# Windowed attention and a gated layer on one core: when attention weights are normalised, turned and read back

## The chip, the cores and the metric

The kernel runs on one core of a Trainium2 chip. The metric is the device time of one execution in microseconds (us). The core has engines with instruction queues of their own: TensorE (PE; its weight loads PEld) for matrix products into PSUM, VectorE (DVE), ScalarE (ACT), GpSimd (POOL), and SyncE (SP), whose queue issues the DMA transfers in the order in which the program wrote them. An engine takes its instructions in order and stops at one whose inputs are not ready.

## What is computed

Attention with two kinds of window (half the heads look at the last 32 keys, the others at every fourth of the last 128), then a gated layer. Cut to what matters:

```python
batch, n_heads, seq, head_dim = (8, 8, 576, 64)        # q, k, v
scores = np.where(masks, scale * q @ k.T, -1e9)
attn = np.exp(scores - max(scores)); attn = attn / (sum(attn) + 1e-09)
x = (attn @ v).transpose(0, 2, 1, 3).reshape(4608, 512)
h = x @ w_in                                           # w_in 512 x 2048
g = h * erf(softplus(h))
out = g @ w_out                                        # w_out 2048 x 512
```

## The kernel before

**Attention** is cut into 72 units. A unit is eight strips of 32 queries, two heads on top of each other, with 64 keys a strip. For each unit TensorE makes the scores (`scores`, L243), VectorE applies the mask and takes the maximum (`mask_max`, L254), ScalarE takes exponents and their sums (`exponents`, L264), VectorE forms the reciprocal of the sums and POOL multiplies by it (`normalize`, L275 to L277). The product with the values needs the weights turned, keys along the partitions. Units up to 17 are turned on TensorE (`turn`). Units from 18 (`LATER`) are turned another way: VectorE transposes 32x32 blocks of two units into `pT` (`swap`, L309), one DMA puts the result into DRAM (`pt<-pT`, L312, "the put"), and one DMA a unit reads it back, regrouped, into the unit's `prob` tile (`back`, L321, `prob<-pt`, "the load back"). The load back cannot go out before its put has landed. The value products (`later_values`, L332) read it.

**The layer** runs over chunks of 512 tokens. The first three chunks are done plainly, in the plain part: a loop over 48 half steps `x`, two to a pair of 128 hidden columns (`t`, `j`). A half step is, on TensorE, twelve products of the first matrix (`mm1`, L590) into PSUM bank `h` (even half steps) or `tx` (odd ones), then twelve of the second matrix two pairs behind (`mm2`, L705). VectorE copies the bank out (`take`, L662), ScalarE applies softplus and erf, VectorE multiplies and splits the result into a high and a low part (`gate`: L674, L680 `ghi`, L681 `glo`), which the `mm2` of the next half step reads. The remaining chunks come behind the plain part, in periods, which the change does not touch.

**Visits** put attention work into the loop. `visits` gives each half step its units: from half step 13 on, every odd half step up to 41 takes two units (9 takes two as well, 11 none). At the end of a visited half step TensorE does `attend`: value products of the pair whose scores were made two visits before, scores of the new pair; then ScalarE copies rows out (L386). SP gets, behind it, the next values and queries (`load_v`, L231, `load_qk`, L224), and the stores of finished rows (`store_x`, L416) and of other results.

**The way of a pair before**, with the visit in half step x: mask and maximum at its end, exponents in x + 1, normalised by VectorE and POOL in x + 2, transposed and put in x + 3, read back at the very end of x + 3, used by the visit of x + 4. Lists hold the units on the way: `todo`, `fresh` and `scaled` (to be normalised), `divided` (to be transposed), `away` (to be read back). Between the put and the load back in SP's queue stands whatever that half step issues, in half steps 8 to 22 the load of weights (`load_w`, L493, called by `prep_dve` inside `weights` once VectorE has emptied the buffer). In half step 28 `fetch_x` issues eight loads of activations (L577) early in the half step. From half step 29 on, `build` makes sums of weights for the later part (L600 to L629), with its stores (L604, L629) on SP. In half step 11 (`SAVED`) `pT` is used for something else.

Of the kernel before, what the change touches and what calls it, by code (L numbers as in the profile page):

```python
# [62 lines left out]
NT = len(STEPS)  # L63
# [9 lines left out]
SAVED = 2 * (HALF + 1) + 1  # L73
# [21 lines left out]
LATER = 2 * NBLK  # L95
# [67 lines left out]
def attn_moe_kernel(ctx: ExitStack, tc: tile.TileContext, qk, v, masks, eye, w_in, w_out, out):  # L163
# [57 lines left out]
    def load_qk(u):  # L221
        if u < NU:
            n = QW + key_start(u, SPU - 1) + KEYS
            nc.sync.dma_start(out=qkz[u % 2][:, 0:n], in_=qk[u, :, 0:n])  # L224
# [46 lines left out]
    def normalize(u):  # L271
        rinv = small.tile([P, 2 * PARTS], F32, name="rinv")

        if u >= FIRST:
            nc.vector.tensor_scalar(sums[u], sums[u], 1.0e-9, None, op0=ALU.add)  # L275
        nc.vector.reciprocal(out=rinv, in_=sums.pop(u))
        nc.gpsimd.tensor_tensor(probs[u], probs[u], rinv.broadcast_to([P, 2 * PARTS, KEYS]), op=ALU.mult)  # L277
        if u >= LATER:
            divided.append(u)
# [19 lines left out]
    def swaps():  # L299
        if divided:  # L300
            swap(list(divided))
            divided.clear()

    def swap(units):

        m = len(units)
        t = pz[1][:, 0:m * 2 * P].rearrange("p (b u n) -> p b u n", b=2, u=m)
        for i, u in enumerate(units):
            nc.vector.transpose(out=t[:, :, i].rearrange("p b (g q) -> p g b q", g=2 * PARTS),  # L309
                                in_=probs[u].rearrange("p g (b k) -> p g b k", b=2))  # L310
        put = dram.tile([2, P, m, P], F32, name=f"pt{units[0]}")
        nc.sync.dma_start(out=put.rearrange("s (r b) u n -> (s r) (b u n)", b=2),  # L312
                          in_=t.rearrange("p b u n -> p (b u n)"))
        away.extend((u, put[:, :, i]) for i, u in enumerate(units))
# [3 lines left out]
    def back():  # L318
        while away:
            u, put = away.pop(0)  # L320
            nc.sync.dma_start(out=probs[u].rearrange("p (s g) k -> p s (g k)", s=2),  # L321
                              in_=put.rearrange("s p n -> p s n"))
# [95 lines left out]
    def has(u):  # L418
        return 0 <= u < NU
# [3 lines left out]
    def busy(k):  # L423

        for _ in range(k):
            nc.tensor.matmul(h, idle[:, 0:P], idle, start=True, stop=True)

    def first_visit(n):

        m = n - LAG  # L430
        copy = nc.scalar.copy if 1 <= n <= EARLY else nc.vector.tensor_copy
        if has(m):
            transposes(m)
        scores(n)
        load_qk(n + 2)
        busy(2 if has(m) else 6)
        if has(m):
            turned(m, copy)
        if 1 <= n <= EARLY:
            prep_act()  # L440
        if has(m):
            values(m)
            busy(2)
        if has(n - 2):
            normalize(n - 2)
        mask_max(n)
        part_lo()
        if has(m):
            rows(m)
            finish(m)  # L450
        if m == NBLK - 1:
            part_lo()
        exponents(n)
        load_v(n - 1)
# [34 lines left out]
    def load_w(i):  # L489
        if prep:  # L490
            _, src, hi, lo = prep.pop(0)
            d = doubles(i)
            nc.sync.dma_start(out=d, in_=src.bitcast(I32).rearrange("p (n w) -> p n w", w=2))  # L493
            staged.append((i, d, hi, lo))
# [346 lines left out]
    for p in (1, 2, 3):  # L841
        j = i - 13 + p
# [542 lines left out]
    with tc.manual_schedule():  # L1385
        nc.gpsimd.memset(idle, 1.0)
        busy(8)
        load_qk(0)
        nc.sync.dma_start(out=cst[:, 0:NMASK * KEYS], in_=masks)
        load_qk(1)  # L1390
        nc.sync.dma_start(out=ident, in_=eye)
        for n in range(FIRST):
            if n < 3:
                load_w(n)
            first_visit(n)
            if 1 <= n <= EARLY:
                prep_dve()
        normalize(FIRST - 2)
        part_lo()

        plan, late = visits()


        pause = SAVED + 1,

        def weights(x):
            if x not in pause:
                prep_act()
                prep_dve(keep=2 if SAVED - 4 < x <= SAVED else None)

        due = {n - LAG: x for x, ns in plan.items() for n in ns if n < LATER + LAG}
        todo, scaled, fresh = [], [FIRST - 1], []
        for x in range(2 * NT):
            t, j = divmod(x, 2)
            ns = plan.get(x, [])
            scored, ready = [n for n in ns if has(n)], ready_of(ns)
            second.update(ready[1:])

            if t < 2:
                turn(ready)  # L1420
                weights(x)
            if t < NT:
                after = STEPS[t + 1][0] if ends(t) and t + 1 < NT else None
                if x == 2 * HALF - 4:
                    load_x(1, range(twice))
                elif x == 4 * SPC - 4:
                    fetch_x(2)
                if x == SAVED:
                    hold(True)
                mm1(t, j)  # L1430
                if x == 0:
                    for cc in range(twice, CC):
                        nc.sync.dma_start(out=x0[cc - twice], in_=xs[cc].bitcast(F32)[:, :, 0:TOK])
                part_lo()
                if not late_take(t, j):
                    take(t, j)
                if after is not None and j == PAIR - 1:
                    load_x(after, range(twice, CC))
                    part_lo()

            if x == 1 or j == 0 and x:
                for u in todo:
                    exponents(u)
                fresh, todo = todo, []
            if late_take(t, j):
                take(t, j)
            if j == 1 and 1 <= t <= NT:
                table(t - 1)
            if t < 2:
                attend(ready, scored)  # L1450
            if t >= 2:
                turn(ready)
                if j == 0 and x < 2 * NT - 4:
                    swaps()

            while scaled:
                normalize(scaled.pop(0))
            scaled, fresh = fresh, []
            if j == 1 and 1 <= t <= NT:
                gate(t - 1, 0)  # L1460
            if j == 0 and 2 <= t:
                gate(t - 2, 1)
            if j == 1 and t < NT:
                argument(t)
            if t >= 2:
                if x != SAVED:
                    weights(x)
                mm2(t - 2, j)
                if x == SAVED:
                    save()  # L1470
                    weights(x)
                    hold(False)
                    load_w(2)
                elif ends(t - 2):
                    if j == 1:
                        store(STEPS[t - 2][0])
                    elif STEPS[t - 2][2] == 2:
                        fetch()
            if t >= 2:
                attend(ready, scored)  # L1480
            def at_once():
                for u in [u for u in scaled if due.get(u) == x + 1]:
                    scaled.remove(u)
                    normalize(u)

            def load_units():
                for n in ns:
                    soon(load_v, n - 1 - (n >= LATER + LAG))
                    soon(load_qk, n + 2)

            sooner = BUILD <= x < PACE[-1]
            if sooner:
                load_units()
            load_left(t + 2, j)
            jobs(FORE.get(x, ()))
            build(x, at_once if x > BUILD else (lambda: None))
            if not sooner:
                load_units()
            back()
            for n in scored:  # L1500
                mask_max(n)
                todo.append(n)
            if x == 4 * SPC - 2:
                load_x(2, range(twice))
            at_once()
            for m in ready:
                finish(m)
        assert not todo and not scaled and len(divided) <= 2
        for i in range(len(ITEMS)):
            period(i, late)  # L1510
        for d in range(FIN * SPC, DOUBLES * SPC):
            final(d)
        rest_steps()
        for s in range(len(LASTS)):
            sums_step(s)
        assert not pending and not prep and not staged and not begun and not made and not rest
# [86 lines left out]
```

## Time and profile before

| | before |
|---|---|
| median of 3 runs | 910.04 us (906.52 to 912.1) |
| profiled execution: its own time | 910.9 us |
| its span, first to last instruction | 909.1 us |
| TensorE busy | 861.3 us (95%) |
| VectorE, ScalarE, POOL busy | 696.0, 608.3, 87.3 us |
| mean granted clock of TensorE, as a share of full speed | 0.983 |
| moved by DMA | 207.72 MB, 228 GB/s |

The profile is of one execution. "A <- B" in a wait means that A stood idle until B was done. Matrix products are pipelined, so a line of several shows the time they occupy together. Times in the rows below are counted from the start of the span.

### The profile page before, as it was taken

What the parts mean: (1) busy time and instruction counts of PE and PEld (TensorE: products, weight loads), DVE (VectorE), ACT (ScalarE), POOL (GpSimd) and SP (SyncE); (2) the same over time, 40 slices, a digit from 0 to 9 for tenths busy, and PEclk for the clock granted to TensorE, in tenths of its full rate; (3) what the DMA queues carried; (4) which work ended last, traced back from release to release, by engine and by line L of the source; (5) the groups of instructions that cost most, each with busy time, mean ns of one, the idle gap of its engine ahead of it and who ended that gap; (6) DMA issues with size and microseconds to landing.
All of it is one profiled execution on the core that took longest, in us unless ns stands there. A gap on an engine that the chain in (4) does not pass through costs nothing.

```text
span 909.1 us, 21921 instructions
## 1 busy us (share of the span) xinstructions
PE 861.3 (95%) x8302; PEld 707.4 (78%) x8314; DVE 696.0 (77%) x1748; ACT 608.3 (67%) x1358; POOL 87.3 (10%) x97
## 2 busy tenths in 40 slices
PE   7799899889979799999999999999999999999998
PEld 3467788677867678878888878888788888889998
DVE  5888888768658688978677767586788768878895
ACT  6889879776858578766676843567456547776442
POOL 2322111112111111001111100010000000000000
PEclk9999999989989899999999999999999999999999
DMA  8874446465648979867786792567668638999541
GB/s 288 286 258 135 150 155 223 150 212 160 214 154 275 314 234 329 310 202 266 264 264 228 252 319 93 160 252 246 203 192 285 240 115 312 324 315 379 187 147 47
DMA packets 102425, 207.72 MB, mean 228 GB/s; under 512 B 10416, under 2 KB 41648, under 8 KB 99248
## 3 DMA queue, kind: packets, MB, share of 16 engines
q1 hardware_dynamic: 99360, 197.88, 64.8%
q10 hardware_dynamic: 2960, 8.46, 2.3%
q8 instruction: 65, 1.06, 0.5%
q14 instruction: 40, 0.33, 0.1%
HBM read 141.54 MB, written 64.75 MB: 227 GB/s over the span
## 4 chain that ended last, share of the span: by engine, by line
PE 49%; DVE 2%; DMA 2%; issue 0%; ACT 0%; SPq 0%; DVEq 0%
PE acc L705 16%; PE h L865 8%; PE tx L865 8%; PE sp L865 6%; PE acc L1231 4%; PE sp L1231 2%; PE tx L1231 1%; PE h L1231 1%; PE sp L332 1%; DMA win<-xT 1%; PE sp L243 1%; DMA prob<-pt 1%; DMA out_dram<-w 1%; DVE glo L681 0%; DVE rows L1062 0%
## 5 line engine op out<-in xcount | busy, mean ns | idle before, releaser
L705 PE MATMUL acc<-wout_hi,ghi 128*128 128x512 f32 x448 | 174.9, 391 | 0.2 <-DVE o L744 0.2
L705 PE MATMUL acc<-wout_lo,ghi 128*128 128x512 f32 x448 | 174.4, 389 | 0.0
L705 PE MATMUL acc<-wout_hi,glo 128*128 128x512 f32 x448 | 123.8, 389 | 1.6 <-DVE glo L681 1.6
L277 POOL TENSOR_TENSOR prob<-prob,rinv 128x256 f32<-128x256 f32 x72 | 77.6, 1092 | 494.0 <-DVE ssum L275 326.5
L264 ACT ACTIVATE prob<-prob,nmax 128x64 f32<-128x64 f32 x288 | 96.3, 337 | 7.9 <-DVE nmax L254 4.1
L705 PEld LDWEIGHTS acc<-wout_hi,glo 128*128 128x128 f32 x448 | 84.0, 188 | 19.5 <-DVE glo L681 2.0
L705 PEld LDWEIGHTS acc<-wout_hi,ghi 128*128 128x128 f32 x448 | 84.1, 188 | 18.6 <-DVE ghi L680 0.7
L705 PEld LDWEIGHTS acc<-wout_lo,ghi 128*128 128x128 f32 x448 | 84.1, 188 | 17.3
L254 DVE CUSTOM_DVE_ANT_0 prob<-sp,cst 128x64 f32<-128x64 f32 x288 | 45.2, 219 | 53.5 <-ACT rows L386 41.2
L914 ACT ACT_TABLE_LOAD x26 | 33.4, 1283 | 46.2 <-DVE hc L882 23.7
L386 ACT COPY rows<-sp 128x128 f32<-128x128 f32 (+7 forms) x167 | 27.6, 306 | 48.2 <-PE sp L243 47.7
L332 PEld LDWEIGHTS sp<-prob,v 64*64 64x64 f32 x1728 | 30.7, 145 | 35.1 <-issue 29.3
L332 PE MATMUL sp<-prob,v 64*64 64x32 f32 x1728 | 33.8, 229 | 24.8 <-DMA prob<-pt 21.1
L865 PE MATMUL tx<-win 128*128 128x512 f32 x216 | 55.9, 394 | 0.2 <-DVE hc L884 0.2
L865 PE MATMUL h<-win 128*128 128x512 f32 x216 | 55.9, 394 | 0.2 <-DVE dbl L884 0.2
L264 ACT ACTIVATION_READ_ACCUMULATOR prob<-prob,nmax 128x1 f32 x288 | 54.4, 189 | 0.0
L590 PE MATMUL h<-x,win 128*128 128x512 f32 x192 | 51.1, 409 | 1.0 <-issue 1.0
L590 PE MATMUL tx<-x,win 128*128 128x512 f32 x192 | 48.0, 392 | 0.0
L865 PEld LDWEIGHTS h<-win 128*128 128x128 f32 x216 | 39.9, 188 | 9.8 <-DVE dbl L884 1.3
L865 PEld LDWEIGHTS tx<-win 128*128 128x128 f32 x216 | 39.9, 188 | 9.6 <-DVE hc L884 0.9
L590 PEld LDWEIGHTS h<-x,win 128*128 128x128 f32 x192 | 37.4, 199 | 9.9 <-issue 1.3
L590 PEld LDWEIGHTS tx<-x,win 128*128 128x128 f32 x192 | 35.7, 188 | 7.5
(312 smaller groups left out, 1912.2 us busy)
## 6 DMA issues: line engine op xcount, KB each, us to landing
win<-ws SPq DMA_DIRECT2D x24, 1024.0 KB, 5.2
v<-in_v_dram SPq DMA_DIRECT2D x72, 256.0 KB, 4.8
win<-ws SPq DMA_DIRECT2D x24, 768.0 KB, 5.8
qk<-in_qk_dram SPq DMA_DIRECT2D x48, 272.0 KB, 4.8
dbl<-in_w_in_dram SPq DMA_DIRECT2D x16, 512.0 KB, 4.3
dbl<-in_w_out_dram SPq DMA_DIRECT2D x16, 512.0 KB, 4.2
ws<-x SPq DMA_DIRECT2D x32, 256.0 KB, 5.2
win<-wd SPq DMA_DIRECT2D x14, 512.0 KB, 8.4
```

Source lines behind the costliest of these rows:

```text
L243: nc.tensor.matmul(sps[h][r * STRIP:(r + 1) * STRIP, i, p, :], qkz[i][hs, s * STRIP:(s + 1) * STRIP], qkz[i][hs, at:at + KEYS], start=True ...
L254: nc.vector.tensor_tensor_reduce(out=pr[:, g, :], in0=sps[h][:, u % 2, p, :], in1=mask[QUADS.index(kinds(u, p))], scale=-SCALE, scalar=HUG ...
L264: nc.scalar.activation(out=probs[u][:, j, :], in_=probs[u][:, j, :], func=AF.Exp, scale=-1.0, bias=nmax[:, j:j + 1], accum_out=sums[u][:, ...
L277: nc.gpsimd.tensor_tensor(probs[u], probs[u], rinv.broadcast_to([P, 2 * PARTS, KEYS]), op=ALU.mult)
L332: nc.tensor.matmul(xp[h * D:(h + 1) * D, qs], vt[ks, s, h, :], w[ks, s % 2, h, s // 2 ^ p, :], start=True, stop=True, tile_position=(p * K ...
L386: nc.scalar.copy(out=to, in_=src)
L590: nc.tensor.matmul((h, bank)[j], win_at[:, ftp, j, cc // 2, w, cc % 2, :], x[cc], start=(k == 0 and i == 0), stop=(k == CC - 1 and i == 2))
L705: nc.tensor.matmul(args["out"], args["lhsT"], args["rhs"], start=args["start"], stop=args["stop"])
L865: nc.tensor.matmul(bank_, w[:, wi, c, :], x[c][:, xi, :], start=(c == 0 and n == 0), stop=(c == 1 and n == 2))
L914: nc.scalar.activation(out=l, in_=e, func=AF.Softplus)
L1231: nc.tensor.matmul(y, x[:, at_], w, start=(q == 0 and j == 0 and n == 0 and s % 2 == 0), stop=(q == QUART - 1 and j == 1 and n == 2), skip ...
```

## The change

Three edits, all in the loop of the plain part. First, in an even half step, units from 18 on are normalised at once, at the end of the half step that made their exponents (x + 1; from half step 30 on ahead of the sums of L609), and no longer after the copy of `tx` in x + 2. Second, `swaps` (the transposes and the put) is called in odd half steps, x + 2, behind that copy; not in half step 11, and not from half step 43 on. A pair visited in half step 9 is therefore put in 13 where it was put in 12. Third, `back` is called in even half steps, x + 3, behind the first products and ahead of `weights`, and no longer as the last but one thing of each half step. The visit that uses the weights stays x + 4.

```diff
             if t >= 2:
                 turn(ready)
-                if j == 0 and x < 2 * NT - 4:
+                if j and x != SAVED and x < 2 * NT - 5:
                     swaps()
+                elif j == 0:
+                    back()
...
             def at_once():
-                for u in [u for u in scaled if due.get(u) == x + 1]:
+                for u in [u for u in scaled if due.get(u) == x + 1 or u >= LATER and j == 0]:
                     scaled.remove(u)
                     normalize(u)
...
             if not sooner:
                 load_units()
-            back()
             for n in scored:
                 mask_max(n)
                 todo.append(n)
```

SP's queue in half steps 16 and 17, as a piece of the difference (- before, + now). `pt_2298` is the put that before went out in half step 16; `pt_2160` is the one of the same pair of units now, put in half step 15; `dbl` are loads of weights:

```order
 L224 DMA qk_83<-in_qk_dram 128x544
 L416 DMA xT_103<-rows 128x576
-L312 DMA pt_2298<-pT_88 128x512
-L493 DMA dbl_2311<-in_w_out_dram 128x1024
-L321 DMA prob<-pt_2298 128x2x128 x2
-L493 DMA dbl_2362<-in_w_out_dram 128x1024
+L321 DMA prob<-pt_2160 128x2x128 x2
+L493 DMA dbl_2313<-in_w_out_dram 128x1024
+L312 DMA pt_2351<-pT_88 128x512
+L493 DMA dbl_2366<-in_w_out_dram 128x1024
```

The load back has come up to right behind the store of rows, ahead of the load of weights, and the next pair's put stands between the two loads of weights.

SP's queue in half step 28, before (a load of activations is the last of eight):

```order
L577 DMA w<-xT_102 128x128
L577 DMA w<-xT_103 128x384
L312 DMA pt_3450<-pT_88 128x512
L321 DMA prob<-pt_3450 128x2x128 x2
L231 DMA v_86<-in_v_dram 128x512
L224 DMA qk_84<-in_qk_dram 128x544
```

and now:

```order
L577 DMA w<-xT_102 128x128
L577 DMA w<-xT_103 128x384
L321 DMA prob<-pt_3293 128x2x128 x2
L312 DMA pt_3494<-pT_88 128x512
L231 DMA v_86<-in_v_dram 128x512
L224 DMA qk_84<-in_qk_dram 128x544
```

The load back passes a put, but the eight loads of activations stay ahead of it.

VectorE in half steps 18 and 19 before, from the copy of bank `h` on (`win` and `w` are the preparing of weights, `ssum` and `rinv` the normalising):

```order
L662 COPY hc<-h 128x512
L309 STREAM_TRANSPOSE pT_88<-prob 128x4x2x32 x2
L680 CAST ghi<-s 128x512
L681 TENSOR_TENSOR glo<-s,ghi 128x512
L522 TENSOR_TENSOR win<-w,win 128x4x128
L526 TENSOR_SCALAR w<-w 128x512
L527 SCALAR_TENSOR_TENSOR w<-dbl_2171,w 128x512
L528 SCALAR_TENSOR_TENSOR w<-dbl_2171,w 128x512
L662 COPY hc<-tx 128x512
L275 TENSOR_SCALAR ssum<-ssum 128x4
L276 RECIPROCAL rinv<-ssum 128x4
```

and now, from the low part `glo` on:

```order
L681 TENSOR_TENSOR glo<-s,ghi 128x512
L522 TENSOR_TENSOR win<-w,win 128x4x128
L526 TENSOR_SCALAR w<-w 128x512
L527 SCALAR_TENSOR_TENSOR w<-dbl_2175,w 128x512
L528 SCALAR_TENSOR_TENSOR w<-dbl_2175,w 128x512
L275 TENSOR_SCALAR ssum<-ssum 128x4
L276 RECIPROCAL rinv<-ssum 128x4
L275 TENSOR_SCALAR ssum<-ssum 128x4
L276 RECIPROCAL rinv<-ssum 128x4
L662 COPY hc<-tx 128x512
L309 STREAM_TRANSPOSE pT_88<-prob 128x4x2x32 x2
L674 TENSOR_TENSOR s<-hc,s 128x1024
```

The normalising has moved ahead of the copy of `tx`, and the transposes from behind the copy of `h` to behind the copy of `tx`, between it and the product `s`.

## Rows read from the trace of the kernel before

**Rows 1.** Waits of TensorE, whole run: waiter, releaser: us in total, times, longest.
```profile
PE sp L332 <- DMA prob<-pt: 21.1, 7, 5.4
PE sp L332 <- issue: 3.4, 2, 2.9
PE h L590 <- issue: 1.0, 1, 1.0
```

**Rows 2.** Timeline of TensorE, value products: start, us, operation, [idle before <-releaser].
```profile
108.16 0.89 PE L332 MATMUL sp<-prob,v 64*64 64x32 f32 x32 [2.87 <-issue]
...
161.80 1.56 PE L332 MATMUL sp<-prob,v 64*64 64x32 f32 x64 [2.89 <-DMA prob<-pt]
...
177.89 1.14 PE L332 MATMUL sp<-prob,v 64*64 64x32 f32 x64 [1.39 <-DMA prob<-pt]
...
194.03 1.93 PE L332 MATMUL sp<-prob,v 64*64 64x32 f32 x64 [3.11 <-DMA prob<-pt]
...
255.30 1.93 PE L332 MATMUL sp<-prob,v 64*64 64x32 f32 x64 [5.44 <-DMA prob<-pt]
...
303.81 1.93 PE L332 MATMUL sp<-prob,v 64*64 64x32 f32 x64 [5.10 <-DMA prob<-pt]
```

**Rows 3.** Busy times by stretch: length, engines' busy us, granted clock, DMA share, GB/s.
```profile
108.16:347.24 239.08, 216.72 (x2657) 177.43 (x2657) 178.37 (x548) 176.80 (x453) 34.52 (x30) 0.94 0.64 211
177.89:194.03 16.14, 13.03 (x177) 10.68 (x177) 13.94 (x41) 12.32 (x33) 2.35 (x2) 0.99 0.60 184
194.03:209.77 15.74, 15.74 (x177) 12.88 (x177) 9.14 (x34) 10.11 (x28) 1.38 (x1) 0.79 0.57 169
223.84:236.81 12.97, 12.97 (x177) 10.65 (x176) 8.81 (x32) 10.22 (x28) 2.35 (x3) 1.00 0.50 149
285.67:303.81 18.14, 13.05 (x176) 10.68 (x177) 14.39 (x40) 11.05 (x28) 2.35 (x2) 0.98 0.89 309
```

**Rows 4.** Timeline of SP's queue, half steps 7, 8, 15 and 16: start, us, transfer issued.
```profile
99.35 0.33 SPq L493 DMA_DIRECT2D dbl<-in_w_in_dram  x1
...
104.52 0.90 SPq L321 DMA_DIRECT2D prob<-pt  x2
...
152.26 0.42 SPq L416 DMA_DIRECT2D xT<-rows  x1
152.77 0.38 SPq L312 DMA_DIRECT2D pt<-pT  x1
...
159.03 0.88 SPq L321 DMA_DIRECT2D prob<-pt  x2
```

**Rows 5.** Lines L321 (first) and L312, 85 to 375 us: landing times.
```profile
DMA to landing us min/median/max: 2.0/2.7/5.8
...
DMA to landing us min/median/max: 1.7/3.8/7.3
```

**Rows 6.** Waits of SP's queue, whole run: us in total, times, longest.
```profile
SPq L321 <- DMA pt<-pT: 29.4, 13, 3.6
```

**Rows 7.** Timelines of VectorE, POOL and TensorE, half steps 15 to 17.
```profile
146.41 0.98 DVE L681 TENSOR_TENSOR glo<-s,ghi 128x512 fp32r<-128x512 f32 x1
...
152.56 0.69 DVE L681 TENSOR_TENSOR glo<-s,ghi 128x512 fp32r<-128x512 f32 x1
...
156.23 0.69 DVE L662 COPY hc<-tx 128x512 f32<-128x512 f32 x1 [0.59 <-PE tx L590]
...
157.47 2.35 POOL L277 TENSOR_TENSOR prob<-prob,rinv 128x256 f32<-128x256 f32 x2 [10.63 <-DVE ssum L275]
...
152.40 1.07 PE L705 MATMUL acc<-wout_hi,glo 128*128 128x512 f32 x4
```

**Rows 8.** Timeline of SP's queue, half steps 28 and 35.
```profile
246.76 2.19 SPq L577 DMA_DIRECT2D w<-xT  x4
249.04 0.38 SPq L312 DMA_DIRECT2D pt<-pT  x1
252.86 0.88 SPq L321 DMA_DIRECT2D prob<-pt  x2
...
300.79 2.12 SPq L746 DMA_DIRECT2D out_dram<-w  x4
```

## The prediction, made before the changed kernel ran

> **What bounds the kernel now.** I read the views in this order. First TensorE's waits: over the whole run it waits 21.1 us, in seven places, for one thing, the load that brings turned attention weights back (`prob<-pt`), and next to nothing else; 2.9 us at the same line are put down to "issue" [rows 1]. All of these lie in the plain part. The timeline then gives the places: the value products (L332) of the visits that start at 108.16 (the "issue" one: its load back was issued only at 104.52), 161.80, 177.89, 194.03, 255.30 and 303.81 us, and two more that share the remaining 3.2 us [rows 1, 2, 4]. Then busy times from visit to visit. A visit comes every second half step; where nothing is late, as from 223.84 us, two half steps take 12.97 us and TensorE is busy for all of it [rows 3]. So TensorE sets the pace, and a wait of TensorE is paid in full. The stretches show a second loss. Behind the wait of 1.39 us the granted clock is 0.99 over the stretch; behind the one of 3.11 us it is 0.79, and the stretch takes 15.74 us with TensorE busy throughout, 2.77 us too long [rows 2, 3]. That is time at the lower level (1.2 GHz in place of 2.4); the clock fell only after the long waits.
>
> **How much there is to win.** From 108.16 to 347.24 us, the first and the last visit of the plain part that read returned weights, there are 16 pairs of half steps. Fourteen should take 14 x 12.97 = 181.6 us. The first two pairs hold one visit, with half the value products (12.97 less half of 1.14 is 12.4, and 12.97 less a visit of 1.95 is 11.0): 23.4. Together 205.0, and they take 239.08: 34.1 too long. With the first wait, 2.87, the loss is 37.0 us: 24.0 of waits for the load back, 1.0 for another load (L590), and 12 of low clock [rows 1, 2, 3].
>
> **What the change moves.** Nothing is added or taken away: each pair of units keeps two normalisations, two multiplies on POOL, two transposes, one put (256 KB) and two loads back (128 KB each), and TensorE's order stays. Three things move.
>
> *The load back.* In half step 16 before, the put goes out at 152.77, a load of weights stands behind it, and the load back goes out at 159.03; TensorE, free at 161.80 - 2.89 = 158.91, starts at 161.80 [rows 2, 4]. Now that visit's put has gone out a half step earlier, and the load back stands right behind the store of rows (L416) issued at 152.26: it goes out at about 152.7, 6.3 us sooner. That is 6.8 us after the visit that starts at 145.87. The second load follows 0.4 us later and lands 2.7 us after issue in the median, 5.8 at worst [rows 4, 5]: 9.9 to 13.0 us after the visit's start, needed 12.97 after it. At most other visits L416 goes out sooner than here. So six of the seven waits and the low clock behind them go (the seventh, at 255.30: below). For the first visit the load goes out behind the weights of 99.35, at 99.7 instead of 104.52, so that it lands at 103 to 106.4, with 105.29 needed: it goes as well.
>
> *The put.* The transposes now follow the copy of `tx`, some 10 us after a visit, and the put is issued some 12 us after it; it takes 3.8 us in the median, 7.3 at worst [rows 5], so it has landed at 16 to 19. The load back asks for it at about 17 to 20. I cost this at nothing. If the put were late, SP would stand at the load back, as it did before for 29.4 us over the run [rows 6], and now the load of weights, the next put and the next values would stand behind it. The Trainium skill's page "DMA: Bandwidth & Descriptors" (section Anatomy of one DMA) says just this: a wait in front of a DMA is spent on the issuing sequencer. The trace agrees by that row. [...]
>
> *VectorE and POOL.* Normalising costs VectorE what it did, but at the end of an even half step, ahead of the copy of `tx`, where it idles (0.59 us at 156.23, more elsewhere). The transposes go from the even to the odd half step. New is that they can meet POOL: its two multiplies take 2.35 us, started at 157.47 and would now start 1.2 us sooner (0.59 of idle, 0.61 of copy), at 156.3; they end at 158.6, and the first transpose could begin at 156.9. So VectorE waits up to 1.3 us before the second, in the four or five visits with weights to prepare. What hides it: the part of `s` that TensorE reads at 152.40 was ready at 147.4, 5 us ahead [rows 7]. I take nothing; without that cover it would be 5 x 1.3 = 6.5 us. Against it stands a small gain: beside the multiply `glo` takes 0.98 us, without it 0.69 [rows 7], and it no longer lies beside it. The page "GPSIMD Engine Reference" (section 1, Specifications) of the Trainium skill speaks of interfaces to SBUF that POOL shares with VectorE. By that rule the multiply will slow the weights' steps or the sums of L609 instead and the gain is nil; these rows agree as far as they go. Neither reaches TensorE.
>
> **What stays late.** The visit at 255.30: in half step 28 eight loads of activations (L577) are issued ahead of the load back in both versions, the last four from 246.76 to 248.95; the load back only passes the put, from 252.86 to 249.0 [rows 8]. With 0.9 us for its two issues and 2.0 to 4 of landing it is there at 252 to 254, and needed at 255.30 - 5.44 = 249.86: I take 3.0 us of wait (2 to 4) and 2.2 of low clock behind it, between nothing behind 1.39 us and 2.8 behind 3.11 [rows 2, 3]. The visit after 303.81: TensorE, free at 298.71 there, would reach it at 311.7. Four stores of output (L746) now lie right ahead of that visit's loads, until 302.91 [rows 8]; with values, queries, three L604 and L416 at 0.4 to 0.5 us each behind them the load back goes out near 308 and lands at 311 to 314: 1.2 us (0 to 2.8). For the other visits after 271 us, where transfers are slowest, 1.0 together. That is 3.0 + 2.2 + 1.2 + 1.0 = 7.4, and L590's 1.0 stays.
>
> **The sum.** 37.0 - 1.0 - 7.4 = 28.6 us. The profiled execution took 910.9 us in all (span 909.1), so 882.3; from the median of the timed runs, 910.04, it would be 881.4. I say **882 us**. The part behind is unchanged and TensorE hardly waits there, so it should keep the gain.
>
> **The rivals.**
> - *All of it.* The two late visits are in time too, or late by less than pulls the clock down: 910.9 - 36 = 875 us. For it: loads back often land in 2.0 to 2.7 us. Against: eight loads lie ahead in half step 28.
> - *The crowd on the DMA engines.* In the stretch from 285.67 us they are 0.89 busy at 309 GB/s [rows 3]. The same bytes in 13.0 us instead of 18.14 would be 431 GB/s. So transfers spill into the next stretches, landings grow to 5 to 7 us, and the load back is 1 to 3 us late at three to five visits, with low clock behind some: 10 to 15 us given back, 892 to 897.
> - *A pace set by VectorE.* In the stretch before 194.03 it is busy 13.94 of 16.14 us, more than the 12.97 it will have; but part of that is work left over from the wait before, and in a quiet stretch it is 8.81 [rows 3]. If it is the bound while weights are prepared, five stretches lose 1 to 2 us and some later ones up to 1: about 895. Against it: 5 us of lead.
> - *Nothing to measure.* The put, not the load back, turns out late, and the waits only move: 1.5 to 3 us stay at most visits with low clock behind: 903 to 910. For it: SP stood up to 3.6 us at a time for the put [rows 6]. Against: the put goes out 5 us sooner, too.
> - *Slower.* SP's wait for the put holds the load of weights and what follows it. The weights' place in the queue is reached shortly before VectorE frees their buffer, so from a put that takes over 9 us every microsecond goes to them, and with about 6 us more TensorE waits for weights with the clock down. Seven pairs of half steps that lose 6 us each, 42 against 28.6 gained: 924. The slowest put so far, 7.3 us, does not reach that point.
>
> **How the numbers follow.** The forecast, 878 to 888: 0.50. All of it: 0.15. The crowd: 0.15. VectorE: 0.06. Nothing to measure: 0.10. Slower: 0.04. The time is that of the likeliest, 882. For 8 in 10 the range goes from 873 to 897 and leaves out the last two. About 1% (9 us) is what a measurement of this kernel tells from no change: faster 0.86, same 0.10, slower 0.04.
>
> **What would show it.** Right: in TensorE's waits `prob<-pt` falls from 21.1 us in seven places to 3 to 6 in two or three, the longest at the visit of half step 29; two half steps take 13.0 us almost everywhere, at a granted clock of 1.00; the load back is issued within 0.5 us behind L416. A wait of the transposes (L309) for POOL of up to 1.3 us appears while TensorE is untouched. Wrong: waits left at most visits (landing times over 5 us would mean the crowd, a wait of SP for the put the put), a wait of TensorE for `ghi` or `glo`, or a later part that gives the time back.

## The result, and the profile after

The changed kernel takes **881.15 us** (median of 4 runs, 879.38 to 883.27) against 909.1 us for the kernel before on the same chip (4 runs, 906.52 to 912.1): a ratio of 0.9692, 95% interval 0.9653 to 0.9732. The forecast was 882 us, 873 to 897. The profiled execution took 882.08 us, span 880.3 us, mean granted clock 0.992 (0.983 before); TensorE is busy 856.4 us, 97% of the span.

TensorE's waits over the whole run, as in [rows 1]. Of the load back two waits are left where there were seven, and the wait at L590 is gone:

```profile
PE sp L332 <- DMA prob<-pt: 4.4, 2, 2.3
PE sp L332 <- issue: 0.5, 1, 0.5
```

TensorE's timeline at the value products, as in [rows 2]. The visits from half step 13 to 27 (130.22 to 221.10) stand 12.98 us apart without a wait; the two waits are those of half steps 29 and 37:

```profile
106.83 0.67 PE L332 MATMUL sp<-prob,v 64*64 64x32 f32 x32
130.22 1.13 PE L332 MATMUL sp<-prob,v 64*64 64x32 f32 x64
...
221.10 1.14 PE L332 MATMUL sp<-prob,v 64*64 64x32 f32 x64
236.19 1.14 PE L332 MATMUL sp<-prob,v 64*64 64x32 f32 x64 [2.03 <-DMA prob<-pt]
...
290.52 1.93 PE L332 MATMUL sp<-prob,v 64*64 64x32 f32 x64 [2.34 <-DMA prob<-pt]
306.36 1.14 PE L332 MATMUL sp<-prob,v 64*64 64x32 f32 x64
319.32 1.13 PE L332 MATMUL sp<-prob,v 64*64 64x32 f32 x64
```

Busy times by stretch, columns as in [rows 3]. The first row is the whole way from the first to the last of these visits, 239.08 us before. The last two are the stretches behind the two waits:

```profile
106.83:319.32 212.49, 208.12 (x2658) 170.72 (x2657) 176.25 (x553) 179.28 (x456) 18.22 (x30) 0.98 0.70 238
130.22:143.22 13.00, 13.00 (x177) 10.65 (x176) 11.61 (x38) 11.80 (x31) 1.18 (x2) 1.00 0.66 225
236.19:249.15 12.96, 12.96 (x177) 10.65 (x177) 9.04 (x34) 10.52 (x29) 1.37 (x2) 1.00 0.59 191
290.52:306.36 15.84, 15.84 (x177) 12.96 (x177) 9.80 (x34) 10.72 (x31) 1.23 (x2) 0.79 0.79 281
```

The two profiled runs differ by 910.9 - 882.08 = 28.8 us. Of this, 239.08 - 212.49 = 26.6 lie between the first and the last visit, 1.3 ahead of it (108.16 to 106.83) and 0.9 behind it (909.1 - 347.24 = 561.9, 880.3 - 319.32 = 561.0). The gain is kept to the end.

SP's queue in half steps 15 to 17, as in [rows 4]. The load back stands right behind the store of rows (L416), the next put 5.5 us behind it:

```profile
142.01 0.33 SPq L312 DMA_DIRECT2D pt<-pT  x1
...
149.06 0.38 SPq L416 DMA_DIRECT2D xT<-rows  x1
149.54 0.99 SPq L321 DMA_DIRECT2D prob<-pt  x2
152.32 0.34 SPq L493 DMA_DIRECT2D dbl<-in_w_out_dram  x1
154.99 0.33 SPq L312 DMA_DIRECT2D pt<-pT  x1
```

Landing times from 85 to 360 us, L321 first, then L312, as in [rows 5]. Loads back became slower (median 2.7 to 4.8 us), puts faster (3.8 to 2.7):

```profile
DMA to landing us min/median/max: 3.2/4.8/6.0
...
DMA to landing us min/median/max: 2.0/2.7/5.6
```

VectorE and POOL at the same place, as in [rows 7]. POOL's two multiplies now lie where VectorE has no work and waits for `tx`, and take 1.19 us where they took 2.35; the transposes behind them wait for nothing:

```profile
152.68 0.18 DVE L276 RECIPROCAL rinv<-ssum 128x4 f32<-128x4 f32 x1
153.59 0.69 DVE L662 COPY hc<-tx 128x512 f32<-128x512 f32 x1 [0.74 <-PE tx L590]
154.20 0.76 DVE L309 STREAM_TRANSPOSE pT<-prob 128x256 f32<-128x256 f32 x2
...
156.56 0.69 DVE L681 TENSOR_TENSOR glo<-s,ghi 128x512 fp32r<-128x512 f32 x1
...
152.84 1.19 POOL L277 TENSOR_TENSOR prob<-prob,rinv 128x256 f32<-128x256 f32 x2 [11.79 <-DVE ssum L275]
```

### The profile page after: what moved, and what is told of

It is laid out like the page before. It is cut to its first block, busy times and chain, and to the rows that moved or that the text cites. A ratio compares the mean times of both kernels' runs of the same rounds, so it can differ in the third digit from the quotient of the medians.

```text
span 880.3 us, 21936 instructions
## 1 busy us (share of the span) xinstructions
PE 856.4 (97%) x8314; PEld 701.2 (80%) x8314; DVE 690.8 (78%) x1748; ACT 609.4 (69%) x1358; POOL 67.4 (8%) x97
## 4 chain that ended last, share of the span: by engine, by line
PE 54%; DVE 1%; issue 0%; ACT 0%; DVEq 0%
PE acc L705 19%; PE h L865 9%; PE tx L865 8%; PE sp L865 6%; PE acc L1231 4%; PE sp L1231 3%; PE tx L1231 1%; PE h L1231 1%; PE sp L332 1%; PE sp L243 1%; DVE rows L1062 0%; DVE glo L681 0%; DVE dbl L882 0%; DVE dbl L898 0%; DVE hc L918 0%
## 5 line engine op out<-in xcount | busy, mean ns | idle before, releaser
L277 POOL TENSOR_TENSOR prob<-prob,rinv 128x256 f32<-128x256 f32 x72 | 58.2, 819 | 493.4 <-DVE ssum L275 317.5
L590 PE MATMUL h<-x,win 128*128 128x512 f32 x192 | 49.3, 399 | 0.0
L590 PE MATMUL tx<-x,win 128*128 128x512 f32 x192 | 47.9, 392 | 0.0
L590 PEld LDWEIGHTS h<-x,win 128*128 128x128 f32 x192 | 35.9, 190 | 8.2
L590 PEld LDWEIGHTS tx<-x,win 128*128 128x128 f32 x192 | 35.7, 188 | 7.5
L914 ACT ACTIVATE s<-dbl 128x1024 f32<-128x1024 f32 x22 | 23.4, 1062 | 25.4 <-DVE dbl L882 25.3
L332 PEld LDWEIGHTS sp<-prob,v 64*64 64x64 f32 x1728 | 28.6, 138 | 14.9 <-issue 14.9
```

The costliest lines, as they stand in the source:

```text
L332: nc.tensor.matmul(xp[h * D:(h + 1) * D, qs], vt[ks, s, h, :], w[ks, s % 2, h, s // 2 ^ p, :], start=True, stop=True, tile_position=(p * K ...
L590: nc.tensor.matmul((h, bank)[j], win_at[:, ftp, j, cc // 2, w, cc % 2, :], x[cc], start=(k == 0 and i == 0), stop=(k == CC - 1 and i == 2))
L914: nc.scalar.activation(out=l, in_=e, func=AF.Softplus)
```

## The experiments

Three moves make the change: the earlier normalising, the earlier put, and the earlier place of the load back in SP's queue. The theory: the gain is the lateness of the load back and nothing else, and of the three moves the earlier place of the load back brings most. The rivals: the earlier put brings it; the normalising brings something of its own; the load back still costs through traffic. Diffs are against the changed kernel. All seven results beside the kernel before on the same chip (medians 910.58 us for the first four, 909.26 for the last three):

| | median us | ratio, 95% interval | first to last visit, us | waits for the load back |
|---|---|---|---|---|
| changed kernel | 881.15 | 0.9692 (0.9653 to 0.9732) | 212.49 | 4.4 in 2 |
| load back last again | 891.86 | 0.9780 (0.9757 to 0.9804) | 219.03 | 9.2 in 7 |
| put late again | 911.45 | 1.0004 (0.9975 to 1.0033) | 238.55 | 21.5 in 8 |
| normalising early alone | 905.50 | 0.9946 (0.9908 to 0.9984) | 232.42 | 18.9 in 7 |
| two visits mended | 876.53 | 0.9613 (0.9588 to 0.9638) | 205.01 | none |
| no load back | 876.24 | 0.9643 (0.9610 to 0.9676) | 205.17 | none |
| put behind the next loads | 907.71 | 0.9980 (0.9955 to 1.0005) | 232.59 | 15.4 in 8 |
| normalising late again | 892.23 | 0.9820 (0.9775 to 0.9865) | 219.03 | 7.8 in 4 |

**The load back last again** (normalising and put early).

```diff
                     swaps()
-                elif j == 0:
-                    back()
...
             if not sooner:
                 load_units()
+            if j == 0:
+                back()
```

> Edit: normalising and put stay early as in the changed kernel, the load back goes to the end of the even half step again, behind the load of weights and the stores of sums. My theory (the place of the load back in SP's queue makes most of the gain): it goes out about 3 us later than in the changed kernel, lands 0 to 3 us too late at half of the visits, TensorE's waits for it add up to 8 to 16 us with low clock behind some: 887 to 898 us, I say 891. If only the put's date counted, it would stay at 881 (within 3); if the put's date were worth nothing, it would be back at 909.

Measured 891.86 us, as expected: 19 of the 28 us (by the medians) stay. SP's queue shows what the load back is behind here:

```profile
152.83 0.38 SPq L416 DMA_DIRECT2D xT<-rows  x1
156.42 0.33 SPq L493 DMA_DIRECT2D dbl<-in_w_out_dram  x1
156.84 0.90 SPq L321 DMA_DIRECT2D prob<-pt  x2
```

It goes out right behind the load of weights, 4 us behind the store of rows, and TensorE waits for it at seven visits, four times for less than 1 us and at most for 3.7. What the early place of the load back is worth once the put is early, some 9 us, is this.

**The put late again** (normalising and put where they were; the load back right behind the put, ahead of the weights).

```diff
-                if j and x != SAVED and x < 2 * NT - 5:
+                if j == 0 and x < 2 * NT - 4:
                     swaps()
-                elif j == 0:
                     back()
...
-                for u in [u for u in scaled if due.get(u) == x + 1 or u >= LATER and j == 0]:
+                for u in [u for u in scaled if due.get(u) == x + 1]:
```

> Edit: normalising and put at their old places (put in the even half step x + 3), the load back right behind the put, ahead of the load of weights. My theory: SP stands at the load back until the put has landed, 2.5 to 4 us, and the load lands 13 to 15 us after the visit where 12.97 is needed: waits of 0.5 to 2.5 us at most visits, some low clock: 886 to 902 us, I say 893. The rival that the queue standing for the put is harmful in itself (weights late, TensorE waits for them) gives over 905 and waits of TensorE other than for the load back.

Measured 911.45 us: a miss. I expected 17 us of gain from the place of the load back; it brings nothing while the put is late. SP's queue in half step 16, and SP's waits from 85 to 360 us (us in total, times, longest):

```profile
150.78 0.38 SPq L312 DMA_DIRECT2D pt<-pT  x1
156.68 0.89 SPq L321 DMA_DIRECT2D prob<-pt  x2
157.66 0.42 SPq L493 DMA_DIRECT2D dbl<-in_w_out_dram  x1
```

```profile
SPq L321 <- DMA pt<-pT: 64.4, 17, 6.3
```

With the load of weights out of the way, SP stands at the load back until the put has landed, 5.9 us here. Summed over the 13 puts of half steps 16 to 40, the time from the issue of the put to the issue of its load back is 58.7 us, and in the kernel before it was 58.0: the place of the load back was not what made it late, the put was. The trace of the kernel before shows it too. Of those 58.0 us the puts needed 55.0 to land, and SP stood for them at 11 of the 13 loads back. At half step 16, the prediction's example, the put took 6.2 us to land; the load of weights went out meanwhile, and SP then stood for the put (152 to 160 us):

```profile
SPq L321 <- DMA pt<-pT: 3.0, 1, 3.0
```

What stands behind the load back in the queue is late in its turn: TensorE's wait at L590, 0.95 us before [rows 1], is 2.54 here.

**Normalising early alone** (put and load back at their old places).

```diff
-                if j and x != SAVED and x < 2 * NT - 5:
+                if j == 0 and x < 2 * NT - 4:
                     swaps()
-                elif j == 0:
-                    back()
...
             if not sooner:
                 load_units()
+            back()
```

> Edit: only the normalising is early; put and load back at their old places. My theory: nothing waited for the normalising, so 909 us, between 905 and 912, with the seven waits for the load back as before. A rival that VectorE's order is worth something by itself (POOL no longer beside the splitting into high and low part) gives 900 or less.

Measured 905.5 us, 5 us under the kernel before (1.5 to 8.4 by the interval), at the edge of what was expected and more than the nothing that I had costed. POOL's multiplies over the whole run, as a group (busy, mean ns of one), before and here:

```profile
L277 POOL TENSOR_TENSOR prob<-prob,rinv 128x256 f32<-128x256 f32 x72 | 77.6, 1092 | 494.0 <-DVE ssum L275 326.5 <-DVE rinv L276 132.3 <-DMA pt<-pT 12.1
```

```profile
L277 POOL TENSOR_TENSOR prob<-prob,rinv 128x256 f32<-128x256 f32 x72 | 59.3, 836 | 514.8 <-DVE ssum L275 328.1 <-ACT prob L264 53.8 <-DVE rinv L276 48.4
```

They take 18 us less, and VectorE is busy 691.7 us where it was 696.0. The waits for the load back fall from 21.1 to 18.9. From the first to the last visit the run is 6.7 us shorter, and 4.9 of these lie at two visits: the wait of half step 21 falls from 3.11 to 1.78 us and the stretch behind it from 15.74 to 14.49, the wait of half step 29 from 5.44 to 4.67 and its stretch from 15.84 to 14.28. Why the load back comes sooner there was not followed.

```profile
192.07 1.14 PE L332 MATMUL sp<-prob,v 64*64 64x32 f32 x64 [1.78 <-DMA prob<-pt]
192.07:206.56 14.49, 14.49 (x177) 11.78 (x177) 10.26 (x34) 10.11 (x28) 1.19 (x2) 0.88 0.61 185
```

**Two visits mended.** In half steps 27 and 35 the load back goes out right behind the stores of output, ahead of the values and queries of the next visit, and so ahead of the eight loads of activations of half step 28.

```diff
                     if j == 1:
                         store(STEPS[t - 2][0])
+                        back()
```

> Edit: the changed kernel, and in half steps 27 and 35 the load back goes out right behind the four stores of output, so ahead of the eight loads of activations in 28 and ahead of values, queries and sums in 35. My theory: the waits of 2.0 and 2.3 us that were left and the 2.9 us of low clock go: 874 us, between 872 and 877, TensorE not waiting for the load back at all. If the crowd on the DMA engines makes them, moving the issue helps little: 879 to 881, with landings over 5 us.

Measured 876.53 us, inside the expected range, and the fastest of those that do all the work. SP's queue in half step 27 here, and the stretch from the first to the last visit:

```profile
219.78 0.33 SPq L312 DMA_DIRECT2D pt<-pT  x1
...
223.12 1.43 SPq L746 DMA_DIRECT2D out_dram<-w  x3
224.66 0.95 SPq L321 DMA_DIRECT2D prob<-pt  x2
```

```profile
106.80:311.81 205.01, 205.01 (x2658) 168.30 (x2657) 175.49 (x552) 178.94 (x456) 18.21 (x30) 1.00 0.73 246
```

The put had landed when the load back asked for it 4.9 us later. TensorE is busy for the whole stretch at a granted clock of 1.00, in the 205.0 us that the prediction worked out as the least.

**No load back.** It leaves out the loads back of the plain part, so that the value products read weights that were never turned; everything else stays.

```diff
                 elif j == 0:
-                    back()
+                    away.clear()
```

> Leaves out the loads back in the plain part: the value products there read weights that were not turned. It is the floor of what earlier loads can give. My theory (all that is left of these waits is two visits): 874 us, as the kernel with these two visits mended, within 2 us. If loads back also slow other work by crowding the DMA engines, it is 870 or less.

Measured 876.24 us, the same as with the two visits mended. Once in time, 33 loads back (4.3 MB) cost nothing that can be measured, neither by their issue nor by traffic. There is nothing left to gain from them.

**The put behind the next loads.** The transposes stay early, but the put's DMA goes out at the end of the odd half step, behind the values and queries of the next visit. (Line numbers from the put on are 4 higher: L325 is the load back, L336 the value products.)

```diff
-        nc.sync.dma_start(out=put.rearrange("s (r b) u n -> (s r) (b u n)", b=2),
-                          in_=t.rearrange("p b u n -> p (b u n)"))
+        send = lambda: nc.sync.dma_start(out=put.rearrange("s (r b) u n -> (s r) (b u n)", b=2),
+                                         in_=t.rearrange("p b u n -> p (b u n)"))
+        if plain_part[0]:
+            unsent.append(send)
+        else:
+            send()
...
             if not sooner:
                 load_units()
+            while unsent:
+                unsent.pop(0)()
```

> Edit: the changed kernel, but the put is issued only at the end of its odd half step, behind the next values and queries (5 to 8 us later); transposes and load back stay. It tests whether the put has room and what a late put does to SP's queue. My theory: SP now stands at the load back for the put, 2 to 4 us, the load lands 11 to 15 us after the visit: waits of 0 to 2 us at a third to half of the visits: 884 to 896 us, I say 889. If the put had no room at all, each visit would lose 4 us or more: over 905. If it has 5 us of room or more everywhere: 881.

Measured 907.71 us: a miss, and past the 905 from which I had said that the put has no room. Nearly the whole gain is gone with 7 to 8 us of delay (at half step 15 the put goes out at 149.76 instead of 142.01). SP's queue at the visit of half step 15, SP's waits from 85 to 360 us, and the put's landing there:

```profile
149.33 0.38 SPq L224 DMA_DIRECT2D qk<-in_qk_dram  x1
149.76 0.42 SPq L312 DMA_DIRECT2D pt<-pT  x1
...
155.82 0.89 SPq L325 DMA_DIRECT2D prob<-pt  x2
```

```profile
SPq L325 <- DMA pt<-pT: 69.8, 16, 5.3
```

```profile
DMA to landing us min/median/max: 4.0/5.3/6.9
```

Two things add up. The put is late, and behind four loads it also takes 5.3 us in the median instead of 2.7. So SP stands for it at nearly every visit, as with the put late. This profiled run is 6.5 us shorter than before from the first to the last visit but 4 us longer behind it (905.5 - 339.56 = 565.9), 1.7 of them waits of TensorE for `ghi`; for `glo` it waits 2.7 us there, 1.6 before; the rest of the 4 us I did not trace.

**Normalising late again** (put and load back early, with the normalising back behind the copy of `tx`, right ahead of the transposes).

```diff
-                if j and x != SAVED and x < 2 * NT - 5:
-                    swaps()
-                elif j == 0:
+                if j == 0:
                     back()
             while scaled:
                 normalize(scaled.pop(0))
             scaled, fresh = fresh, []
+            if t >= 2 and j and x != SAVED and x < 2 * NT - 5:
+                swaps()
...
-                for u in [u for u in scaled if due.get(u) == x + 1 or u >= LATER and j == 0]:
+                for u in [u for u in scaled if due.get(u) == x + 1]:
```

> Edit: the changed kernel, but the normalising goes back into the odd half step, right ahead of the transposes, which then wait for POOL on VectorE in every visit. The put goes out about 2.5 us later. My theory: VectorE's waits for POOL appear, 1 to 2 us at each visit, TensorE does not see them, as the split of s has 5 us of lead and the put has room: 881 to 884 us. The rival that VectorE sets the pace gives 890 or more, with TensorE waiting for ghi or glo.

Measured 892.23 us, 8 us over the expected range's end. The expected wait of VectorE for POOL is there (from 106 to 330 us), but TensorE does not wait for what VectorE makes. It waits for the load back:

```profile
DVE pT L309 <- POOL prob L277: 9.1, 14, 0.8
```

SP's wait at the put for the transposes (85 to 360 us), the put and the load back of half steps 27 and 28, and the visit that reads it:

```profile
SPq L312 <- DVE pT L309: 61.0, 14, 9.0
...
225.09 0.33 SPq L312 DMA_DIRECT2D pt<-pT  x1
...
237.80 0.89 SPq L321 DMA_DIRECT2D prob<-pt  x2
...
242.19 1.93 PE L332 MATMUL sp<-prob,v 64*64 64x32 f32 x64 [4.37 <-DMA prob<-pt]
```

The same put and load back in the changed kernel:

```profile
219.89 0.33 SPq L312 DMA_DIRECT2D pt<-pT  x1
...
232.33 1.02 SPq L321 DMA_DIRECT2D prob<-pt  x2
```

The path is SP. Counted from the visit of half step 27 (224.78 us here, 221.10 in the changed kernel) the put of that half step goes out at +0.31 instead of -1.21, since SP stands at it for the transposes (61.0 us from 85 to 360 us, 45.6 in the changed kernel), and what is behind it is late too: the load back goes out at +13.0 instead of +11.2. The wait of the visit that reads it, in half step 29, grows from 2.03 to 4.37 us, and the stretch behind it takes 15.82 us at a granted clock of 0.79. Of the 6.5 us by which this run is longer from the first to the last visit, this visit is 2.3 + 2.9. The profiled run as a whole is 9.3 us longer; the other 0.5 ahead of the first visit and 2.3 behind the last were not followed.

## Why the prediction was right, and where its parts were not

**The time** came out as forecast, 882.08 against 882.3 us for the profiled run, and the sum's frame held: 37.0 us to win, by a floor of 205.0 that two experiments reach. Two of its parts were wrong and cancelled; that it came within 0.3 us is luck.

**The load back** went out 0.5 us behind the store of rows, as worked out, and six of the seven named waits went. The seventh, at half step 29, fell from 5.44 to 2.03 us, and the visit of half step 37 has a new one of 2.34, both where the prediction put them. The first wait of 2.87 us went too, but the first visit came only 1.3 us sooner: TensorE was 1.5 us later already at 72 us, ahead of anything the change touches.

**The put.** I costed its move at nothing and counted the 6.3 us that the load back moved up. The experiments show that the put's date comes first: put and normalising early without the load back gain 19 us, the load back alone nothing, all together 28. (The put alone with the normalising late, and the load back with the normalising but without the put, were not tried.) The prediction had all three moves, so its sum holds, but it looked for the gain in the wrong one. It read the 6.3 us at half step 16 as the load of weights in between, though [rows 6] showed SP standing for the put; 3.0 of them were that wait. "It has landed at 16 to 19" after a visit was on the safe side: the put shown goes out at 142.01 - 130.22 = 11.8, as worked out, and with the median of 2.7 us in place of 3.8 it is there at 14.5. From 85 to 360 us SP stands for it nowhere. The Trainium skill's page "DMA: Bandwidth & Descriptors" (section Anatomy of one DMA), by which a wait in front of a DMA is spent on the issuing sequencer, agrees with 64.4 and 69.8 us of SP's time in the two experiments whose put was late.

**The late visits** are where the errors were.
- Half step 29: 3.0 of wait and 2.2 of low clock were forecast. It waited 2.03, and the clock stayed at 1.00 behind it. The place was right: eight loads ahead, as the mended version shows. The 2.2 stood between nothing behind a wait of 1.39 us and 2.8 behind one of 3.11, as if the loss grew with the wait; the runs show that it does not go by the length of the wait alone (last section).
- Half step 37: 1.2 was forecast. It waited 2.34 with 15.84 - 12.98 = 2.86 of low clock behind it, 5.2 together. The wait lies inside the 0 to 2.8 that I gave, but the term was mis-sized twice. The load back went out at 285.24, 10.1 us after the visit ahead of it (I had worked out 308 - 298.71 = 9.3), and was there 5.3 us later, at the slow end of the 3 to 6 that I allowed. And I gave this wait no low clock. The stretch ahead shows the DMA engines busy throughout, at 350 GB/s; at this one visit the rival of the crowd may have been right in part, though the mended version, which only issues the load back sooner, has no wait there.

```profile
285.24 1.37 SPq L321 DMA_DIRECT2D prob<-pt  x2
...
275.13:290.52 15.39, 13.05 (x178) 10.69 (x177) 14.13 (x42) 12.10 (x33) 1.23 (x2) 1.00 1.00 350
```

- The other visits behind 271 us: 1.0 was forecast, nothing came. L590's 1.0, which I let stand, went. I take it to have been SP's lateness too: it grew to 2.54 and 3.45 us in the two versions in which SP stood longest, and the loads of `x` for these products (L544) stand behind the load back in the queue.

Forecast 7.4 + 1.0 = 8.4 to stay, found 2.0 + 5.2 = 7.2. The 1.2 us between are about made up by the later start (1.5 us), and what comes behind the last visit is 0.9 shorter.

**VectorE and POOL.** I expected a wait of up to 1.3 us for POOL in four or five visits and no gain. From 106 to 330 us there is one wait, of 0.2 us. The step that failed took 2.35 us for POOL's multiplies, which is their time beside VectorE's two-input operations (`s` from 157.40 and `glo` from 159.38 us in the kernel before); moved into VectorE's wait for `tx` they take 1.19. By the rule of the page "GPSIMD Engine Reference" (section 1, Specifications) of the Trainium skill, interfaces that the two share, I let the contention move elsewhere. The rule agrees with the two durations, but here the contention was not moved, it was gone: `glo` takes 0.69 us instead of 0.98, and POOL's total falls from 87.3 to 67.4 us. The early normalising is worth 5 us alone and, by the version with it late again, about 11 on top of the other two moves, there, as far as it was traced, by the date of the put.

**The rivals.** A pace set by VectorE, nothing to measure and slower are out: TensorE waits for no load back at the other visits. The crowd is out as a general cost, since leaving the loads back out is no faster than having them in time. The 875 us of "all of it" is what the mended version reaches (875.05 in its profiled execution).

## What to carry to other kernels

When a transfer is read back through DRAM, look at the date of the outgoing half first: an earlier place for the return gains nothing unless the put has landed ahead of it; without that it only stalls the queue. On one in-order queue each transfer's place is a price for all behind it, so put what is needed soonest ahead of bulk loads and behind nothing that waits for a compute engine. Once the first 28 us were won, the rest lay in two half steps with other traffic ahead in the queue, and one line won it.

## What the runs showed of the hardware

- Two POOL multiplies of 128x256 f32 take 1.19 us where VectorE waits and then copies, and 2.35 us beside its two-input operations [rows 7].
- The length of a wait alone does not tell what the clock costs behind it. In the changed kernel a wait of 2.03 us left the granted clock at 1.00, and one of 2.34 us was followed by 0.79, 2.86 us of loss. But a wait of 2.04 us with the normalising late again, and one of 2.12 us with the load back last, were each followed by 0.88 with TensorE busy throughout, 1.4 us longer than 12.97; and with the normalising early alone a wait of 1.78 us was followed by 0.88 too, 1.5 us of loss (its rows stand there). In the kernel before, the clock was at 0.98 to 1.00 behind the waits of 1.39 to 1.76 us and fell behind those of 2.87 us and more, which the prediction read as the long waits. The wait of 2.04 us, its stretch, and the stretch behind the 2.12 us:

```profile
299.04 1.13 PE L332 MATMUL sp<-prob,v 64*64 64x32 f32 x64 [2.04 <-DMA prob<-pt]
299.04:313.38 14.34, 14.34 (x177) 11.68 (x177) 9.22 (x35) 11.26 (x32) 1.18 (x2) 0.88 0.91 321
...
242.89:257.23 14.34, 14.34 (x176) 11.68 (x177) 9.10 (x34) 10.52 (x29) 1.55 (x2) 0.88 0.55 174
```

- The same put of 256 KB takes 2.7 us in the median behind the copy of `tx` and 5.3 behind four loads of values and queries; the same loads back take 2.2 us right behind a put that SP waited for and 4.8 among other transfers.
